# A delta rule and a SwiGLU block on one core: the products of chunk 2 in the merged form

## The chip, the cores and the metric

The kernel runs as one program on one core of one Trainium2 chip. The metric is the device time of an execution in microseconds (us). The kernel before was run three times: 691.24 us in the median, 690.71 to 693.55. A further execution was taken with the hardware profiler; every row of a profile below is from such an execution. The engines are called PE (TensorE, with PEld for its loading of weights), DVE (VectorE), ACT (ScalarE), POOL (GpSimd) and SP (SyncE, which issues the transfers). L961 is line 961 of the kernel.

## The reference

There are two blocks, one behind the other. The first is a delta rule over 4 × 8 heads, 768 tokens, head size 48. For each head a state S of 48 × 48 is carried from token to token:

```
k_n = k / (norm(k) + 1e-6)
for t in range(768):
    y[t]  = q[t] S
    S     = S + beta[t] * outer(k_n[t], v[t] - k_n[t] S)
```

The result y, with the heads of a token side by side, is x (3072 × 384). The second block is `(silu(x @ w_gate) * (x @ w_val)) @ w_out`, with 384 → 1536 → 384. All is f32.

## The kernel before

**Chunks.** The tokens are cut into NCH = 12 chunks of C = 64 tokens per head. Inside a chunk the recurrence becomes matrix products: K K and its inverse triangular system (made for two chunks at a time: `invert(g)`, joined by `join_1` or `join(g)`), P = the masked product Q K, and from the state S the products K S and Q S. Two heads' halves share the 128 partitions, so that one "product over all heads" is 32 small products (16 heads × 2 batches' halves); the trace shows each f32 product as two records, so 32 products stand as x64.

**The steps of a chunk.** `advance(c)` is a generator with four steps for c of 2 and above:

1. K S is subtracted from v (`vin`). For chunks below `MERGED` (L930, here 3) this is a product of 48 moving columns per head (L991) into the banks px; chunk 2 issues Q S (L944, `q_of_state`) right behind it into the banks py, and DVE subtracts in one instruction (L1001). For chunks from `MERGED` on, the moving operand is Q transposed and the state side by side (`qs`, 64 + 48 = 112 columns): one product per head (L961) gives K Q and K S together, par 0 into px, par 1 into py. DVE subtracts twice (L967) and masks K Q into P three times (L977: once from px, twice 64 partitions from py).
2. For chunks from `MERGED` on, Q S first (into py); then the first solution, `zt` times `r` (L1029, into px), which ACT copies out (`uu`, L1050).
3. The state's update (L1131, added by DVE at L1140) and P times u, which accumulates upon Q S in py (L1119); ACT copies y out (L1176, L1178).
4. y is transposed (L1192) into x of the chunk (`x_ffn`, L1198).

px and py are pairs of PSUM banks, one tile each; K K, K Q, the joins, the products above and the transposes all take turns in them. The other four banks (`ffn`) belong to the second block.

**P of a chunk below `MERGED`.** It is made ahead of the chunk, in `products(k_c, q_c)`, a generator of two steps that serves one chunk's K and one chunk's Q: in the first step both are transposed on PE, in the second `gram` makes K K of chunk `k_c` (L527 into px, copied by ACT at L553 and L556) and then, if `q_c < MERGED`, K Q of chunk `q_c` (L527 into py), which DVE masks (L545) into `p_sb`. Chunk 2's Q goes with chunk 4's K.

**The second block.** For chunks 0 and 1: gate and value products per pair of 128 columns (`gate_val`, L1397), silu on ACT (L1406), the product of both on DVE (L1408), and later the products with w_out (`output`, L1424). From chunk 2 on a form with fewer products is used (`gate_val_fast`, L1301; `output_fast`, L1507), with sums of weights and of x made on DVE (L1465, L1468). While chunks 0 and 1 run, DVE and ACT also convert the weights (`convert`, L289, L297, L309; `power_step`, L272, L278), which arrive in two words a value.

**The order.** It is written out by hand (`tc.manual_schedule`): each engine runs its instructions in the program's order. The second block's loops call `point(c)`, which runs one step: a step of `advance(c)` that has begun, or else a step of preparation (`prep_step`: a join, the second step of `products`, or a new one), or else the first step of `advance(c)`; `may_advance` lets a chunk begin when its P stands (`c in p_sb`) or, from `MERGED` on, its transposed Q (`c in qt`), and when enough steps of its join are done (two for chunk 2). `fill(n)` runs n units of work for DVE: conversions while there are weights left, then steps of `invert`. The list `spent`, in which steps enter what they take of DVE, is read in `point_and_fill` alone, which the products of chunks 2 and above call.

The last loop of the old form is `output(1, 1, fill, range(2, FT, 2))` (L1859): twelve products with w_out (`f`), and ahead of each even one from 2 on `fill(2)`, `point(2)` and `sums_of_w(f)`. The joins of chunk 2 and the steps of `advance(2)` stand there: ahead of f = 2 and 4 the two steps of the join (L809; L821 into py, which ACT copies out at L829), ahead of f = 6, 8 and 10 the first three steps of the chunk, and `finish(2)` behind the loop runs the fourth.

Of the kernel before, what the change touches and what calls it, by code (L numbers as in the profile page):

```python
# [20 lines left out]
def kernel(  # L21
# [539 lines left out]
    def gram(*args):  # L561
        for _ in gram_steps(*args):
            pass
# [363 lines left out]
        yield  # L927

    p_1 = []
    MERGED = 3  # L930

    def advance(c):

# [18 lines left out]

        if c >= MERGED:
            both = [
# [670 lines left out]
    def steps(kind, *args):  # L1625
        return gens.get((kind, args), (None, 0))[1]
# [4 lines left out]
    def products(k_c, q_c):  # L1631
# [6 lines left out]
        if k_c is not None:  # L1638
            gram(k_c, False, None, (nc.scalar.copy, nc.scalar.copy))
            if k_c % 2 == 1:  # L1640
                fills.append((k_c // 2, invert(k_c // 2)))
        if q_c is not None and q_c < MERGED:
            gram(q_c, True)
# [15 lines left out]
    def may_advance(c):  # L1659
        g = c // 2  # L1660
        due = {0: 0, 1: 2 + 2 * (c % 2)}.get(g, 2)
        return steps("advance", c) > 0 or ((c in p_sb or c >= MERGED and c in qt) and steps("join", g) >= due)

# [11 lines left out]
    def prep_step(c):  # L1675
# [19 lines left out]
        next(gen)  # L1695
        if k_c is not None or q_c < MERGED:
            going.append(gen)
# [206 lines left out]
```

## Time and profile before

| | us |
|---|---|
| three executions, median (lowest to highest) | 691.24 (690.71 to 693.55) |
| the profiled execution | 690.57 |
| its span, first to last instruction | 688.5 |
| PE busy in the span | 674.0 |
| DVE, ACT, POOL busy | 416.4, 261.6, 192.6 |
| granted clock of PE, mean | 0.996 of full |

A row of a timeline gives the start and the time it takes in us, the engine, the line, the operation, what it writes and reads, its shape and the number of instructions that the row holds; in brackets stands the idle time ahead of it and what ended that. PE's rows overlap a little, since its instructions are pipelined: the pace is read from one row's start to the next one's. "issue" is time in which the profile shows nothing that was waited for. The chain of waits gives start, length, engine and line of the work that ended last, followed back from the end.

### The profile page before, as it was taken

The page shows a single profiled execution, that of the slowest core. Times are in us where ns is not written, and L with a number is a line of the kernel's source. Part 1 is how long each engine was busy: PE and PEld are TensorE (multiplying, and loading weights), DVE is VectorE, ACT ScalarE, POOL GpSimd, SP SyncE. Part 2 cuts the span into 40 slices and gives each one's busy share as a digit, 9 for nine tenths or more (in the row PEclk, how much of TensorE's full clock was granted, in tenths as well). Part 3 has the DMA queues.
Part 4 walks back from the last instruction along what each step waited for, and adds up shares of the span by engine and source line. Part 5 has one row for each costly group of instructions (what it writes and reads, how often), then busy time and mean ns, then how long its engine had stood idle before and what let it go on. Part 6 is the DMA issues. An engine that isn't in the chain of part 4 may idle for free.

```text
span 688.5 us, 24321 instructions
## 1 busy us (share of the span) xinstructions
PE 674.0 (98%) x10696; PEld 627.2 (91%) x10696; DVE 416.4 (60%) x875; ACT 261.6 (38%) x554; POOL 192.6 (28%) x310
## 2 busy tenths in 40 slices
PE   8899999999999999999999999999999999999997
PEld 4687888667999999999999999999999999999997
DVE  7788788898667665637456556555554544433341
ACT  4776765214432622344233245242144142142230
POOL 5110031007882218810027830308810000000000
PEclk9999999999999999999999999999999999999999
DMA  9578733017650611554432373143143121221210
GB/s 133 147 195 217 222 104 126 13 29 175 136 112 11 131 60 40 112 100 92 95 72 70 74 135 71 55 109 71 56 109 70 55 64 47 56 63 47 73 43 24
DMA packets 143849, 62.23 MB, mean 90 GB/s; under 512 B 122976, under 2 KB 126048, under 8 KB 143744
## 3 DMA queue, kind: packets, MB, share of 16 engines
q1 hardware_dynamic: 141536, 60.19, 37.4%
q8 instruction: 84, 1.38, 0.8%
q10 hardware_dynamic: 2080, 0.39, 0.4%
q14 instruction: 21, 0.17, 0.1%
q0 software_dynamic: 128, 0.10, 0.1%
HBM read 53.58 MB, written 7.08 MB: 88 GB/s over the span
## 4 chain that ended last, share of the span: by engine, by line
PE 91%; ACT 2%; DMA 2%; SPq 2%; issue 1%; DVE 1%; POOL 0%; DVEq 0%; ACTq 0%; POOLq 0%
PE ffn L1301 43%; PE ffn L1507 20%; PE ffn L1397 9%; PE ffn L1424 4%; PE p_px L961 2%; PE p_py L944 2%; PE p_px L1029 2%; PE p_py L1119 1%; PE p_px L1131 1%; SPq L140 1%; DMA h_f<-in_moe_w_gate_dram 1%; PE p_px L527 1%; PE p_py L1192 1%; PE ffn L1058 1%; PE p_px L904 1%
## 5 line engine op out<-in xcount | busy, mean ns | idle before, releaser
L1301 PE MATMUL ffn<-x_ffn,wg_sb 128*128 128x128 f32 x840 | 128.4, 275 | 0.6 <-ACT ffn L1357 0.3
L1301 PE MATMUL ffn<-x_ffn,wv_sb 128*128 128x128 f32 x840 | 128.1, 275 | 0.0
L1301 PEld LDWEIGHTS ffn<-x_ffn,wg_sb 128*128 128x128 f32 x840 | 111.1, 192 | 1.0 <-ACT ffn L1357 0.7
L1301 PEld LDWEIGHTS ffn<-x_ffn,wv_sb 128*128 128x128 f32 x840 | 110.7, 192 | 0.0
L1336 DVE TENSOR_TENSOR h_f<-sil,ffn 128x256 f32<-128x256 f32 x120 | 49.6, 418 | 83.9 <-ACT sil L1331 82.5
L1331 ACT ACTIVATE sil<-ffn 128x256 f32<-128x256 f32 x120 | 46.0, 385 | 128.7 <-PE ffn L1301 126.6
L1507 PE MATMUL ffn<-wo_sb,h_f 128*128 128x192 f32 x480 | 83.4, 327 | 0.0
L843 POOL TENSOR_TENSOR n_b<-mb,half 128x32 f32<-128x32 f32 x5 | 30.1, 6010 | 178.6 <-DVE mb L569 178.6
L1507 PEld LDWEIGHTS ffn<-wo_sb,h_f 128*128 128x128 f32 x480 | 78.1, 190 | 0.3
L599 POOL TENSOR_TENSOR tmp<-zb,mb 128x31 f32<-128x31 f32 (+15 forms) x124 | 68.9, 556 | 16.9 <-DVE mb L586 7.5
L605 POOL TENSOR_TENSOR zb<-zb,tmp 128x31 f32<-128x31 f32 (+15 forms) x124 | 69.6, 561 | 9.7
L1468 DVE TENSOR_TENSOR ffn<-ffn,p_sb 128x512 f32<-128x512 f32 x58 | 40.3, 695 | 48.7 <-ACT ffn L1357 47.3
L1301 PE MATMUL ffn<-x_t,h_f 128*128 128x128 f32 x480 | 61.0, 280 | 0.2 <-ACT ffn L1314 0.2
L1301 PEld LDWEIGHTS ffn<-x_t,h_f 128*128 128x128 f32 x480 | 56.3, 191 | 2.1 <-ACT ffn L1314 0.4
L1468 DVE TENSOR_TENSOR o_sb<-o_sb,ffn 128x192 f32<-128x192 f32 x49 | 17.2, 352 | 63.6 <-PE ffn L1507 60.9
L1314 ACT COPY ffn<-ffn 128x512 f32<-128x512 f32 x30 | 17.1, 571 | 60.7 <-PE ffn L1301 60.7
L1465 DVE TENSOR_TENSOR h_f<-h_f,h_f 128x256 f32<-128x256 f32 x60 | 30.2, 509 | 11.4 <-PE ffn L1507 10.2
L1507 PE MATMUL ffn<-last_k,h_f 128*128 128x192 f32 x200 | 36.0, 327 | 0.0
L1397 PE MATMUL ffn<-x_ffn,wg_sb 128*128 128x256 f32 x144 | 34.5, 385 | 0.4 <-DVE x_ffn L1196 0.3
L1397 PE MATMUL ffn<-x_ffn,wv_sb 128*128 128x256 f32 x144 | 33.8, 382 | 0.0
L1507 PEld LDWEIGHTS ffn<-last_k,h_f 128*128 128x128 f32 x200 | 32.9, 190 | 0.1
L1397 PEld LDWEIGHTS ffn<-x_ffn,wg_sb 128*128 128x128 f32 x144 | 26.5, 190 | 4.8 <-DVE wg_sb L309 0.8
(314 smaller groups left out, 1123.1 us busy)
## 6 DMA issues: line engine op xcount, KB each, us to landing
h_f<-w_s SPq DMA_DIRECT2D x60, 256.0 KB, 2.8
p_sb<-w_s SPq DMA_DIRECT2D x27, 256.0 KB, 2.9
vin<-in_v_dram SPq DMA_DIRECT2D x48, 96.0 KB, 3.3
out_dram<-o_sb SPq DMA_DIRECT2D x48, 96.0 KB, 2.2
kn<-in_k_dram SPq DMA_DIRECT2D x20, 192.0 KB, 4.6
zt<-in_moe_w_out_dram SPq DMA_DIRECT2D x6, 384.0 KB, 4.0
qpad<-in_q_dram SPq DMA_DIRECT2D x36, 64.0 KB, 3.1
w_s<-h_f SPq DMA_DIRECT2D x7, 256.0 KB, 4.4
```

Source lines behind the costliest of these rows:

```text
L599: engine.tensor_tensor(out=t_v, in0=zb[:, 0 : j + 1, j : j + 1].to_broadcast([128, j + 1, m]), in1=mb[:, j : j + 1, j + 1 : R].to_broadcas ...
L605: engine.tensor_tensor(out=zb[:, 0 : j + 1, j + 1 : R], in0=zb[:, 0 : j + 1, j + 1 : R], in1=t_v, op=ALU.add,)
L843: nc.gpsimd.tensor_tensor(out=n, in0=mb.rearrange("p j i -> p (j i)")[:, 0 : R * R : R + 1], in1=half, op=ALU.pow,)
L1301: nc.tensor.matmul(p[:, u], w(u), moving, start=start and u == 0, stop=True, skip_group_check=True,)
L1314: nc.scalar.copy(p_y, p_x)
L1331: nc.scalar.activation(sil[:, n].rearrange("p (i n) -> p i n", i=2), p[:, 0:2], ACTF.Silu)
L1336: nc.vector.tensor_tensor(out=h_of(c, f, j), in0=sil[:, n].rearrange("p (i n) -> p i n", i=2), in1=p[:, 2:4], op=ALU.mult,)
L1397: nc.tensor.matmul(ps[name][:, i], w_sb[:, t, (f + i) * 128 : (f + i + 1) * 128], xts[c][:, t], start=(t == 0 and i == 0), stop=(t == KT - 1),
L1424: nc.tensor.matmul(p_o, hs[c, f - f % 2][:, f % 2, bp * 128 : (bp + 1) * 128], wo_sb[:, f], start=(f == 0), stop=(f == FT - 1),)
L1465: nc.vector.tensor_tensor(out=out, in0=a, in1=b, op=ALU.subtract)
L1468: nc.vector.tensor_tensor(out=out, in0=a, in1=b, op=ALU.add)
L1507: nc.tensor.matmul(p[x, part], a(f - f % 2)[:, f % 2], b(f), start=not begun and f == 0, stop=f == FH - 1, skip_group_check=True,)
```

## The change

Chunk 2 is computed in the merged form, as chunks 3 to 11 are:

```diff
--- before.py
+++ after.py
@@ -927,7 +927,7 @@
         yield
 
     p_1 = []
-    MERGED = 3
+    MERGED = 2
 
     def advance(c):
 
```

`MERGED` is read at four places. In `products`, K Q of chunk 2 is no longer made next to chunk 4's K K, nor masked. In `prep_step` it tells whether the second step of `products` is wanted; with chunk 4's K it is, before and after. In `may_advance`, chunk 2 asks for its transposed Q instead of its P. In `advance(2)`, the first step has the 32 products of 112 columns, two subtractions and three maskings in place of K S, Q S and one subtraction; Q S comes first in the second step, ahead of the first solution. What is computed stays the same.

## The prediction

> **What bounds the kernel now.** I read four views in this order: the page's busy times, the chain of waits, the timelines at the two places that the change touches, and the timeline at chunk 3, which already runs the form that chunk 2 is to get.
>
> ```profile
> PE 674.0 (98%) x10696; PEld 627.2 (91%) x10696; DVE 416.4 (60%) x875; ACT 261.6 (38%) x554; POOL 192.6 (28%) x310
> ```
>
> TensorE is busy for 674.0 of 688.5 us. That is an average, so the two places have to be looked at by themselves. After 171 us the waits of PE add up to only 1.6 us (its longest, 1.1 us, is one of L1301 for DVE): whatever shifts the work before 171 us shifts the end by as much. First place: the chain of waits where chunk 2's P is made today, near 76 us.
>
> ```profile
> 77.97 0.43 DVE wg_sb L309
> 78.40 0.04 issue
> 78.44 35.66 PE ffn L1397 x164
> ```
>
> The chain comes from DVE here, not from PE: the gate products of L1397 wait for a converted weight until 78.44 us and then run without a gap for 35.66 us (and PE stays in the chain to 155 us). The same place in DVE's timeline:
>
> ```profile
> 75.42 0.69 DVE L1408 TENSOR_TENSOR h_f<-sil,ffn 128x512 f32<-128x512 f32 x1 [4.13 <-PE ffn L1397]
> ...
> 78.64 1.28 DVE L545 TENSOR_TENSOR p_sb<-p_py,mask_q 128x512 f32<-128x512 f32 x2
> ```
>
> L1408 starts DVE's chain as soon as the value products end; the masking of P (L545) stands behind the conversion that PE waits for. Second place: the first two steps of chunk 2. First ACT's timeline, then PE's.
>
> ```profile
> 155.63 2.34 ACT L829 COPY zt<-p_py 32x512 f32<-32x512 f32 x4 [2.65 <-PE p_py L821]
> ```
>
> ```profile
> 156.91 1.15 PE L991 MATMUL p_px<-qs,kt 48*64 48x48 f32 x64
> 158.03 0.90 PE L944 MATMUL p_py<-qs 48*64 48x48 f32 x42
> 159.08 0.56 PE L944 MATMUL p_py<-qs 48*64 48x48 f32 x22 [0.16 <-issue]
> 159.57 1.56 PE L1424 MATMUL ffn<-wo_sb,h_f 128*128 128x384 f32 x4
> 161.05 1.15 PE L1029 MATMUL p_px<-vin,zt 64*64 64x48 f32 x64
> ```
>
> PE has no gap to speak of. K S (L991) writes px while ACT still copies out of py; Q S (L944) writes py from 158.03 us, just after the last of these copies ends (155.63 + 2.34 = 157.97). A f32 product stands as two records, so 32 products are x64. Third, chunk 3 in PE's and DVE's timelines:
>
> ```profile
> 193.52 0.31 PE L961 MATMUL p_px<-qs,last_k 48*64 48x112 f32 x1
> ...
> 195.21 2.05 PE L1301 MATMUL ffn<-x_t,h_f 128*128 128x128 f32 x16
> ...
> 199.87 1.15 PE L944 MATMUL p_py<-qs 48*64 48x48 f32 x64
> 200.84 1.11 PE L1029 MATMUL p_px<-vin,zt 64*64 64x48 f32 x64
> ```
>
> ```profile
> 195.33 0.55 DVE L967 TENSOR_TENSOR vin<-vin,p_px 128x384 f32<-128x384 f32 x1 [0.91 <-PE p_py L961]
> ...
> 196.98 1.39 DVE L977 TENSOR_TENSOR p_sb<-p_py,mask_q 64x512 f32<-64x512 f32 x2
> ```
>
> From the first merged product, PE is free after 195.21 - 193.52 = 1.69 us, DVE begins after 1.81 us, and its five instructions end at 196.98 + 1.39 = 198.37, 3.04 us after they began. In chunk 3 PE has 4.66 us of L1301 between the two steps, so nobody sees those 3.04 us.
>
> **The change, part by part.**
>
> *P by itself goes (76 us).* 32 products (x64) on PE, 1.1 us by L527's row at 76.22 us, and two masked copies on DVE, 1.28 us. The step that holds them also makes K K of chunk 4, so it stays a step, and the order of all later steps stays as it is; chunk 2 is let in by the join (two steps of it), not by P, so its start in the order stays too. On the path this is worth 0: PE would come to the gate products 1.1 us sooner, and wait 1.1 us longer for the weight that DVE finishes at 78.40 us. DVE cannot be sooner, for L1408 waits for products ahead of P. The 1.28 us stand behind that conversion, and PE has no wait for DVE from 78.44 to 151 us. The upper bound of the gain is the 1.1 us; I take 0, as the chain has it.
>
> *K S becomes the product of 112 columns (157 us).* It writes px and py in turn, so its second product needs py free, which K S did not: ACT's four copies (L829) hold py until 157.97. PE could begin at 156.91 + some 0.05 and stands until 158.03: 1.05 us of new waiting. Does the half that writes py's first bank have to wait for copies out of the second one too? The nearest row says yes:
>
> ```profile
> 20.78 1.09 PE L511 MATMUL p_py<-ident,last_k 128*128 128x128 f32 x8
> 21.91 1.07 ACT L515 COPY last_k<-p_py 128x512 f32<-128x512 f32 x2 [1.31 <-PE p_py L511]
> ```
>
> There the copy of py's first bank, whose transposes are the first four of eight, began only when all eight were done (20.78 + 1.09 = 21.87). The pair of banks is guarded as one. The Trainium skill (PSUM — Partial Sum Buffer, PSUM bank collisions raise a hardware error) says that guarding bank by bank and quadrant is enough; by that the first half could run under the copies, and the delay below would be 1.9 instead of 2.8 us. The row decides against that here.
>
> *DVE.* One subtraction (0.95 us, L1001) becomes two of 0.55 and three maskings of 0.68 to 0.70: 3.04 us by chunk 3. The merged product's last record ends at 158.03 + 1.77 = 159.80, less some 0.03 for the pair that ran ahead; DVE runs from 159.82 to 162.86. Behind it in DVE's queue stand eight sums of weights (159.30 to 162.07 now, 2.7 us): they end near 165.6, ahead of the state's addition (L1140), which then waits for PE until about 167.5. So they cost nothing; without those 1.9 us of cover they would delay the state. SP stores some of these sums: it is at 167.34 us when it issues the last three, and their sources are done by 165.6, so no transfer is later by more than the shift itself.
>
> *Q S moves behind the masking (second step).* It writes py, so it waits for both maskings that read py: 162.86 + 0.05 = 162.91. PE has only the four records of L1424 (1.49 us) to do meanwhile: 159.70 to 161.19. It stands 1.72 us. Q S then takes 200.84 - 199.87 = 0.97 us, and the first solution (L1029) starts at 163.87 instead of 161.05.
>
> *Sum.* Work of PE between 156.91 and L1029: before 1.12 + 1.54 + 1.48 us, after 1.69 + 1.49 + 0.97, so nothing (4.14 against 4.15). Waits: 1.05 + 1.72 = 2.77. L1029 is later by 2.82 us. Behind it come, now as before, copy, products, y's copies, transposes, x, all in one chain to 171 us, where PE goes on without gaps. **Plus 2.8 us**: the profiled execution's 690.57 us (span 688.5 and 2.1 around it) becomes 693.4. The median shown, 691.24, lies 0.67 above that execution, so the median after is 691.24 + 2.8 = **694.0 us**, 0.4% slower. Bounds of the delay: 1.9 with each bank guarded by itself, less 1.1 if P's 1.1 us count in full, so 0.8; above, 2.8 plus a lost stretch of clock, next.
>
> **The rivals.**
>
> *A slower clock (slower).* PE stands twice within 6 us, the second time for 1.72 us with only 0.3 us of work in the 2 us from 161 on. The trace has one drop: the granted clock is 0.54 from 14 to 16 us, after two microseconds in which PE was busy 0.74 us. Against: from 28 to 30 us it was busy only 0.66 us and the clock stayed 1.00. The drop lasted 3.41 us. L511's transposes went from 272 to at most 447 ns, so in 3.41 us 3.41 × 272 / 447 = 2.08 us of work gets done: 1.3 us lost. Time: 691.24 + 2.8 + 1.3 = 695.4. It decides if the granted clock is under 1.00 anywhere between 160 and 168 us. The Trainium skill (TensorE: Matmul & The Clock Gate, What's actually happening) has the clock halved after an idle window of about 3.4 us that runs freely; the drop's length agrees, and by an entirely idle window neither stand here would suffice.
>
> *Banks guarded one by one (less slower).* The first half runs from 156.97, the second from 158.03 in 0.83 us, DVE 158.95 to 161.99, Q S at 162.04, L1029 at 163.0: plus 1.9, 693.2 us. Against it the row of L515.
>
> *P's removal counts after all.* If PE were not held at 78.44, the 1.1 us would come off: plus 1.7, 692.9 us. The chain speaks against it. To be faster than before, the removed 1.1 and 1.28 us would both have to count and the two waits to vanish (−2.4, 688.8); no row supports it.
>
> **How the numbers follow.** A difference under 0.5% (3.5 us) is about what a measurement of this kernel cannot tell from none. Chances: the plain sum 0.66, the clock 0.18, the two smaller delays 0.12, faster 0.04. The plain sum lies only 0.7 us under the bound, and a stall for instructions in the dense run of Q S and L1029 (0.16 us in the row above, 0.64 us at 47.21 in the same kind of run), or the spread of executions, carries it over: I give 0.30 of its 0.66 to "slower by over 0.5%" and 0.36 to "within". So slower 0.30 + 0.18 = 0.48, within 0.36 + 0.12 = 0.48, faster 0.04. The range takes in 692.9 and 695.4 and some spread of the median: 692.6 to 696.2.
>
> **What would show it.** Right: PE still held until about 78.4 us by L309, with the wait grown to about 1.5 us; L961's second record at about 158.0, behind L829; Q S behind L977 at about 162.9 after an idle PE of 1.7 us; L1131 at about 166.4 instead of 163.62, and the same 2.8 us at every later stage. Wrong: if PE reaches the gate products' third weight before 78.3, if L961 runs through from 157.0, if Q S begins before the maskings end, if the clock falls below 1.00, or if the distance to the kernel before changes after 171 us.

## The result, and the profile after

The kernel after takes 697.93 us in the median of 8 executions (695.05 to 702.89), the kernel before, run between them, 692.11 us (690.71 to 693.57). The ratio is 1.0082, with a 95% interval of 1.0054 to 1.011: slower, by about 5.7 us. The forecast was 694.0 us and its range ended at 696.2, so twice the forecast delay came. The profiled execution of the kernel after took 697.05 us, with a span of 695.3 us against the 688.5 us of the kernel before: 6.7 us more.

The page's busy times say nothing about it; PE has 64 products and as many loads fewer, and is yet busy for 1.1 us more (675.1 against 674.0):

```profile
PE 675.1 (97%) x10632; PEld 626.7 (90%) x10632; DVE 416.2 (60%) x877; ACT 261.2 (38%) x554; POOL 192.9 (28%) x310
```

**The first place, near 76 us.** PE's timeline and the chain of waits of the kernel after:

```profile
77.03 1.16 PE L527 MATMUL p_px<-kt 64*64 64x64 f32 x64
78.12 1.13 PE L1397 MATMUL ffn<-x_ffn,wg_sb 128*128 128x256 f32 x4
80.23 1.99 PE L1397 MATMUL ffn<-x_ffn,wg_sb 128*128 128x256 f32 x8 [0.98 <-DVE wg_sb L309]
```

```profile
79.75 0.43 DVE wg_sb L309
80.18 0.04 issue
80.23 9.98 PE ffn L1397 x45
```

K K (L527) is followed at once by the gate products, which then stand for 0.98 us until DVE's conversion L309 ends at 80.18. K K starts 1.79 us later than in the trace of before (77.03 against 75.24), and the products held by L309 are released 1.79 us later as well (80.23 against 78.44). So nothing is won there. These 1.79 us arose in the part of the program that both kernels share. A second profiled execution of the kernel after stands 0.18 us ahead of the kernel before at 65 us, where this one is 1.79 us behind: it is a difference between executions and not the change.

**The second place, chunk 2.** PE's timeline of the kernel after (the shape behind the names, then xcount, and in brackets the idle time ahead), and below it ACT's and DVE's:

```profile
158.45 0.40 PE L961 MATMUL p_px<-qs,kt 48*64 48x112 f32 x2
159.56 0.31 PE L961 MATMUL p_py<-qs,kt 48*64 48x112 f32 x1 [0.70 <-ACT zt L829]
...
161.25 1.56 PE L1424 MATMUL ffn<-wo_sb,h_f 128*128 128x384 f32 x4
164.51 1.15 PE L944 MATMUL p_py<-qs 48*64 48x48 f32 x64 [1.71 <-DVE p_sb L977]
165.48 1.46 PE L1029 MATMUL p_px<-vin,zt 64*64 64x48 f32 x64
166.86 2.83 PE L1424 MATMUL ffn<-wo_sb,h_f 128*128 128x384 f32 x4
169.63 0.94 PE L1131 MATMUL p_px<-uu,kn 64*48 64x48 f32 x64
```

```profile
157.17 2.34 ACT L829 COPY zt<-p_py 32x512 f32<-32x512 f32 x4 [2.06 <-PE p_py L821]
```

```profile
161.41 0.56 DVE L967 TENSOR_TENSOR vin<-vin,p_px 128x384 f32<-128x384 f32 x1 [1.17 <-PE p_py L961]
...
163.07 1.39 DVE L977 TENSOR_TENSOR p_sb<-p_py,mask_q 64x512 f32<-64x512 f32 x2
```

Both forecast waits are there. The first product goes to px and the second, to py, starts when ACT's copies end (157.17 + 2.34 = 159.51). DVE's five instructions end at 163.07 + 1.39 = 164.46, 3.05 us after they began (forecast 3.04), and Q S follows at 164.51, after 1.71 us of standing (forecast 1.72). Then there is something that the sum did not hold: L1424, whose four records took 1.56 us before, takes 2.83, and the 64 records of L1029 take 1.46 instead of 1.15. The view by stretches shows why (length, then PE, PEld, DVE, ACT and POOL busy, the granted clock, the DMA's share, GB/s):

```profile
162.64:166.06 3.42, 1.71 (x105) 1.55 (x108) 3.34 (x8) 0.00 (x0) 3.42 (x2) 1.00 0.64 143
166.06:169.47 3.41, 3.41 (x41) 1.88 (x32) 1.20 (x4) 0.80 (x1) 0.39 (x1) 0.50 1.03 382
```

The clock is halved for 3.41 us behind a stretch of the same length in which PE was busy for half the time.

The starts of the same instructions in both profiled executions, in us, give the whole account:

| instruction | before | after | later by | what came in between |
|---|---|---|---|---|
| K K of chunk 4, L527 | 75.24 | 77.03 | 1.79 | shared part of the program, spread |
| gate products behind L309 | 78.44 | 80.23 | 1.79 | P's products gone: 0 |
| copies of the join, L829 | 155.63 | 157.17 | 1.54 | |
| first solution, L1029 | 161.05 | 165.48 | 4.43 | the two waits: 2.89 |
| state's update, L1131 | 163.62 | 169.63 | 6.01 | halved clock: 1.58 |
| join, L918, first of two | 241.17 | 247.15 | 5.98 | nothing for 75 us |
| chunk 4's L1119 | 299.03 | 305.47 | 6.44 | a stall inside L918: 0.46 |
| join, L918, second of two | 338.18 | 343.57 | 5.39 | a stall of before is gone: −1.05 |
| end of the span | 688.54 | 695.25 | 6.72 | a stall inside L918: 1.33 |

The last column is a difference of starts; the idle time that the profile puts ahead of one product is shorter (0.28 us of the 0.46, 1.14 of the 1.33). The last three rows lie more than 70 us behind the last instruction that the change touches. In PE's timeline of the kernel before, and then of the kernel after:

```profile
299.03 1.11 PE L1119 MATMUL p_py<-uu,p_sb 64*64 64x48 f32 x64
301.20 1.02 PE L1301 MATMUL ffn<-x_ffn,p_sb 128*128 128x128 f32 x7 [1.05 <-DVE qs L1140]
```

```profile
305.47 1.11 PE L1119 MATMUL p_py<-uu,p_sb 64*64 64x48 f32 x64
306.52 1.16 PE L1301 MATMUL ffn<-x_ffn,p_sb 128*128 128x128 f32 x8
...
343.57 1.17 PE L918 MATMUL p_py<-t,z 32*32 32x32 f32 x115
345.88 0.32 PE L918 MATMUL p_py<-t,z 32*32 32x32 f32 x13 [1.14 <-issue]
```

The kernel before stands for 1.05 us behind chunk 4's L1119; the kernel after does not, but stands for 1.14 us in the middle of 128 equal products of the join, where nothing is waited for. The prediction read the first of these as "one of L1301 for DVE", as the row has it. It is of another kind, as follows.

**Stalls at the border of a block of instructions.** Number PE's records from the start of the program: loads, products and the 125 entries of its sequencer (waits, above all) that the trace holds. The 1.05 us stand at record 10433, the 1.14 us at record 11457; divided by 256, each leaves a remainder of 193. (A product with its load and its wait is up to three records, so the product that the timeline shows behind the stall can be one or two later.) The DMA view has two queues that carry nothing but instructions; one of them moves 16 KB a packet (packets, MB, share of the engines):

```profile
q8 instruction: 83, 1.36, 0.8%
```

PE's 21389 records hold 83 places with the remainder 193, as many as there are packets; the kernel before has 21517 records, 84 such places and 84 packets, and the two counts are equal in every kernel below too. That this queue feeds PE is concluded from these counts. In each of these stalls the packet ahead landed 1.3 to 1.6 us before PE went on. So the theory: PE's program arrives in blocks of 256 records, and PE stalls at a border (a record with the remainder 193) when it gets there before the next block is usable. The change takes 64 loads and 64 products out of the program at 76 us, and moves every border behind it by half a block.

### The profile page after: what moved, and what is told of

Its sections match the earlier page's. It is cut to its first block, busy times and chain, and to the rows that moved or that the text cites. A ratio compares the mean times of both kernels' runs of the same rounds, so it can differ in the third digit from the quotient of the medians.

```text
span 695.3 us, 24196 instructions
## 1 busy us (share of the span) xinstructions
PE 675.1 (97%) x10632; PEld 626.7 (90%) x10632; DVE 416.2 (60%) x877; ACT 261.2 (38%) x554; POOL 192.9 (28%) x310
## 4 chain that ended last, share of the span: by engine, by line
PE 90%; ACT 2%; DMA 2%; SPq 2%; DVE 2%; issue 1%; POOL 0%; DVEq 0%; ACTq 0%
PE ffn L1301 42%; PE ffn L1507 20%; PE ffn L1397 9%; PE ffn L1424 4%; PE p_px L961 2%; PE p_py L944 2%; PE p_px L1029 2%; PE p_px L1131 1%; PE p_py L1119 1%; SPq L140 1%; DMA h_f<-in_moe_w_gate_dram 1%; PE p_px L527 1%; PE p_py L1192 1%; PE ffn L1058 1%; PE p_py L918 1%
## 5 line engine op out<-in xcount | busy, mean ns | idle before, releaser
L1301 PE MATMUL ffn<-x_ffn,wg_sb 128*128 128x128 f32 x840 | 128.4, 275 | 0.5 <-ACT ffn L1357 0.3
L1301 PE MATMUL ffn<-x_ffn,wv_sb 128*128 128x128 f32 x840 | 128.1, 275 | 0.0
L1301 PEld LDWEIGHTS ffn<-x_ffn,wg_sb 128*128 128x128 f32 x840 | 111.1, 192 | 1.0 <-ACT ffn L1357 0.7
L1301 PEld LDWEIGHTS ffn<-x_ffn,wv_sb 128*128 128x128 f32 x840 | 110.7, 192 | 0.0
L1301 PE MATMUL ffn<-x_t,h_f 128*128 128x128 f32 x480 | 61.0, 280 | 0.2 <-ACT ffn L1314 0.2
L1301 PEld LDWEIGHTS ffn<-x_t,h_f 128*128 128x128 f32 x480 | 56.3, 191 | 2.1 <-ACT ffn L1314 0.4
```

The costliest lines, as they stand in the source:

```text
L1301: nc.tensor.matmul(p[:, u], w(u), moving, start=start and u == 0, stop=True, skip_group_check=True,)
```

## The experiments

**The kernel after again, and with PE kept busy in the two waits.** The first kernel is the changed one without an edit. The second adds products that nobody reads (into a bank of the second block, ffn2), one ahead of the merged products, two ahead of Q S:

```diff
+        def keep_busy(n):
+            for _ in range(n):
+                nc.tensor.matmul(ffn_banks[2][:, 0:DM], ident, wo_sb[:, 0])
...
+            if c == 2:
+                keep_busy(1)
...
+            if c == 2:
+                keep_busy(2)
```

This kernel and the next two use a bank of the second block without setting its last 128 columns anew, and a part of chunk 2's result differs for it; the kernels further below that use the bank write these columns too. Apart from what the edits show, the instructions are the same.

> The changed kernel once more, to see what varies. Theory (two waits and the clock): against the kernel before, L1029 starts 2.8 to 2.9 us later than the start of L829 would make it in every execution (1.05 us for ACT's copies of py, 1.72 us for DVE's maskings), and a stretch of halved clock of 3.41 us behind them costs up to 1.6 us more in some executions and nothing in others; so the times spread by 2 us or more, and the median ratio is 1.004 to 1.008. Rival (the layout of the program): the loss is made of stalls for instructions and of the start, spread over the whole span, and is there before 75 us too; then the profile shows less than 2 us of loss between 150 and 171 us.

> The changed kernel with three products more that nobody reads, 128x384 as those of L1424 (0.75 us each): one ahead of the merged product, two ahead of Q S, so that PE works while it would wait. They fit into the two waits (0.75 of 1.05 and 1.49 of 1.72 us), and the waits stay. Theory: no halved clock between 155 and 175 us, L1424's four records take 1.5 us there and not 2.8, the median falls by the clock's share, 1 to 1.6 us, and stands 2.8 us (ratio 1.004) above the kernel before, with a spread like that one's (3 us). Rival (the clock was chance, or drops whatever PE does): the same time and spread as the changed kernel, ratio 1.008.

The kernel after again: 1.0074 (1.0043 to 1.0105), 696.99 us. Kept busy: 1.0052 (1.0024 to 1.0079), 695.91 us. In the profile of the first the waits are the same and the clock is not halved near 165 us, although PE stood for 1.70 us; but a stall stands inside chunk 2's L1119, at record 5313, which leaves 193 as well:

```profile
164.28 1.15 PE L944 MATMUL p_py<-qs 48*64 48x48 f32 x64 [1.70 <-DVE p_sb L977]
...
168.53 0.74 PE L1119 MATMUL p_py<-uu,p_sb 64*64 64x48 f32 x34
170.31 0.68 PE L1119 MATMUL p_py<-uu,p_sb 64*64 64x48 f32 x30 [1.03 <-issue]
```

So the halved clock comes in some executions and not in others. With PE kept busy it is not halved there either, L1029 is later by 2.89 us as without the extra products (here and below counted from the start of the join's copies, L829), and a stall of 0.43 us stands in the same run of L1119. The intervals of the two kernels overlap, so what the clock costs on average these runs do not tell. Both kernels also stall in the second L918 (0.85 and 0.57 us).

**Q S into a bank of its own, then the join's second step too.** In the first kernel chunk 2's Q S and P times u go into ffn0 and ffn2, so that Q S need not wait for the maskings; in the second the join's step (L821) goes there as well, so that the merged products need not wait for L829:

```diff
+        if c == 2:
+            p_y_of = [ffn_banks[n][:, 0 : NB * NJ * D].rearrange(...) for n in (0, 2)]
...
-                    p_y[half_of(b ^ par), par, bp, j],
+                    p_y_of[par][half_of(b ^ par), bp, j],
```

and in the second kernel also

```diff
-        p_j = ps_pair("p_j", tags[1]).rearrange("p e (m i) -> p e m i", i=C)
+        if c == 0:
+            p_j = [ffn_banks[n].rearrange("p (m i) -> p m i", i=C) for n in (0, 2)]
```

> The changed kernel with chunk 2's Q S, and P times u upon it, in two banks of the second block that are free then (ffn0 and ffn2) in place of py, so that Q S needs no masking to be done. Theory: the wait of 1.72 us ahead of Q S goes, L1029 then waits at most for the masking out of px; the first wait (1.05 us) stays; with only one short wait the clock stays full; L1029 about 1.1 to 1.3 us later than in the kernel before, ratio 1.0015 to 1.002. Rival (layout): the same loss as the changed kernel, ratio 1.008.

> As the run with Q S apart, and the second step of chunk 2's join in the same two banks too, so that the merged product need not wait for ACT's copies out of py (L829). Theory: both waits go and the clock stays full; L1029 within 0.3 us of its place in the kernel before, ratio 0.999 to 1.001; then the merged form itself costs nothing and all of the loss is the two waits and what they do to the clock. Rival (layout, or DVE's 3.04 us are the cost wherever they stand): ratio 1.004 or more.

Q S apart: 1.0032 (1.0015 to 1.0049), 693.95 us; L1029 is later by 1.11 us, the first wait alone. Both apart: 1.003 (1.0015 to 1.0045), 694.45 us; L1029 is within 0.3 us of before. Both ratios lie above what was expected, the second clear of it. So each wait goes when its bank is another. Between the kernel after again and Q S apart the ratio falls by 0.42%, where the second wait alone is 1.71 us or 0.25%; their intervals just overlap. But with no wait left the kernel is still 0.3% slower, some 2 us. PE's timeline of the kernel with both apart shows where they are:

```profile
167.41 0.74 PE L1132 MATMUL ffn<-uu,p_sb 64*64 64x48 f32 x34
169.12 0.67 PE L1132 MATMUL ffn<-uu,p_sb 64*64 64x48 f32 x30 [0.97 <-issue]
...
342.06 1.17 PE L922 MATMUL p_py<-t,z 32*32 32x32 f32 x115
344.36 0.32 PE L922 MATMUL p_py<-t,z 32*32 32x32 f32 x13 [1.14 <-issue]
```

They are the records 5313 and 11457 again, after the same 34 and 115 products of their runs, and the 1.05 us of before at 300 us are gone: 0.97 + 1.14 − 1.05 = 1.06 us, about half of the 2 us. Start to start, with short pauses near 243 and 247 us, it is more: this profile stands 2.97 us behind the one of before at L1029 and 5.19 us at the end, so 2.2 us came behind L1029. With Q S apart the stall in L918 is 1.67 us, and the clock is halved behind it:

```profile
340.02:343.43 3.41, 1.74 (x132) 1.59 (x129) 0.68 (x2) 0.33 (x1) 0.00 (x0) 1.00 0.58 77
343.43:346.84 3.41, 3.41 (x19) 3.41 (x18) 2.39 (x3) 1.06 (x2) 0.21 (x1) 0.50 0.60 106
```

**The removed records put back, unread.** The changed kernel, with the 32 products K Q of chunk 2 still issued at 76 us and read by nobody. The waits stay; from chunk 2's second step on, every border lies where it lay before the change:

```diff
+    def idle_gram(n):
+        p_v = [... for p in banks("p_g", "py")]
+        for bp, j, par, b, _ in list(every())[:n]:
+            nc.tensor.matmul(p_v[par][half_of(b), bp, j],
+                kt[2][half_of(par), bp, j, b], qt[2][half_of(par), bp, j, b])
...
+        elif q_c == 2:
+            idle_gram(32)
```

> The changed kernel, with the 32 products that the change takes away near 76 us still issued there (into py, read by nobody, no masking), where PE waits for DVE anyway. From the end of chunk 2's second step on, PE has then issued as many instructions as in the kernel before. Theory (blocks of instructions: 128 records fewer shift the borders of the fetched blocks into other dense runs of small products): the gap inside chunk 2's L1119 (0.4 to 1.0 us, or hidden by a slow clock) and the one inside L918 near 344 us (0.6 to 1.7 us) are gone, the gap behind chunk 4's L1119 near 300 us (1.05 us in the kernel before) is back; L1029 is still 2.8 to 2.9 us late; ratio 1.004 to 1.006 against 1.0074 to 1.0082 for the changed kernel. Rival (the gaps come from the waits or the merged form): the same gaps as in the changed kernel, the same ratio.

1.0034 (1.0021 to 1.0048), 695.05 us. With more work the changed kernel is faster, not slower: 1.0082 and 1.0074 without these products, 1.0034 with them, a little below the 1.004 to 1.006 expected (the interval of the first, from 1.0054, lies apart; that of the second just overlaps; the runs from here on are from another chip, where the kernel before was run in between as well). L1029 is later by 2.89 us, so what is left is the waits. The stalls in chunk 2's L1119 and in L918 near 344 us are gone, and the one behind chunk 4's L1119 is back, shorter, as before under the name of DVE:

```profile
303.67 1.11 PE L1130 MATMUL p_py<-uu,p_sb 64*64 64x48 f32 x64
305.23 1.13 PE L1312 MATMUL ffn<-x_ffn,p_sb 128*128 128x128 f32 x8 [0.44 <-DVE qs L1151]
```

**Both together.** No wait (as both apart) and next to no shift (as just now); a small product behind Q S (L1013) sets ffn2's last columns anew, which shifts the borders by four records:

> Both waits taken away (Q S and the join's second step of chunk 2 in ffn0 and ffn2) and the 32 unread products kept near 76 us; one small product more behind Q S (128 columns of ffn2, read by nobody). Theory (waits, clock and blocks are all of the loss): ratio 0.9985 to 1.0015, L1029 within 0.5 us of its place in the kernel before, gaps of PE behind 150 us as in the kernel before. Rival (something of the merged form is still dearer): 1.003 as without the unread products.

1.0004 (0.9986 to 1.0022), 692.61 us: the time of the kernel before. One stall of 0.41 us stands in chunk 2's join, at record 4801. The one of 1.05 us behind chunk 4's L1119, which was expected back, is not there, although the borders lie only four records off: L1148 (L1119's place) runs through, and so does the join near 340 us:

```profile
156.66 0.21 PE L836 MATMUL ffn<-t,d_o 32*32 32x32 f32 x1 [0.41 <-issue]
...
301.14 1.11 PE L1148 MATMUL p_py<-uu,p_sb 64*64 64x48 f32 x64
302.18 1.16 PE L1330 MATMUL ffn<-x_ffn,p_sb 128*128 128x128 f32 x8
...
339.22 1.29 PE L933 MATMUL p_py<-t,z 32*32 32x32 f32 x128
```

This is the main result: the slowdown has two parts that can each be undone by itself, the waits (1.0034 where they alone are left) and the shift (1.003 where it alone is left), and undone together nothing is left that can be measured. The last step by itself, from 1.003 to 1.0004, is not clear of the intervals, which overlap; what tells the two apart is where the stalls stand. It is no better than the kernel before either, and none of the versions tried was. Their sum, 0.64%, stands against the 0.74 and 0.82% of the changed kernel.

**P's work taken out of the kernel before, and nothing else.**

```diff
             for bp, j, par, b, _ in every():
+            if of_q and c == 2:
+                continue
```

> The kernel before, with chunk 2's K Q and its two maskings left out and nothing else changed (chunk 2 then uses chunk 1's P, so the output is another from chunk 2 on). It prices the removal by itself. The prediction's step: 0, since PE waits for DVE until 78.4 us in either case; the wait there grows by about 1 us. Theory of the blocks: the removal alone shifts the borders, so there are other gaps behind 150 us than in the kernel before, worth between -1 and +1.5 us in the sum, and none of it at 76 us. Rival (P's 1.1 us count): 1.1 us faster from 80 us on, ratio 0.9985.

1.0007 (0.9989 to 1.0026), 694.01 us against 692.78: no gain from 1.1 us less on PE and 1.28 us less on DVE. PE's timeline shows the same wait for L309 as in the kernel after, and two stalls of blocks in chunk 2:

```profile
79.39 1.99 PE L1401 MATMUL ffn<-x_ffn,wg_sb 128*128 128x256 f32 x8 [0.98 <-DVE wg_sb L309]
```

```profile
162.91 0.66 PE L1033 MATMUL p_px<-vin,zt 64*64 64x48 f32 x26 [0.58 <-issue]
...
167.46 0.67 PE L1123 MATMUL p_py<-uu,p_sb 64*64 64x48 f32 x30 [0.97 <-issue]
```

A third, of 1.17 us, stands in L918 at 341.4 us, and that of before at 300 us is gone. By these rows the kernel should be 0.58 + 0.97 + 1.17 − 1.05 = 1.67 us slower (0.24%), which the interval still holds. The ratio alone would also allow that P's removal wins a little and the stalls take it back; the row of 79.39 is what speaks against that. This kernel has the same shift as both apart and no waits, and its ratio is 1.0007 against 1.003: how much the shift costs in the median is known only roughly.

**Padding and a busy PE.** The padded changed kernel, with unread products in the waits once more, to ask again for the clock:

> The changed kernel with the 32 unread products near 76 us and with unread products in both waits (one of 384 columns ahead of the merged product, one of 384 and one of 512 ahead of Q S), so that neither the clock nor the blocks differ much from the kernel before and only the two waits are left. Theory: L1029 2.8 to 2.9 us late, no halved clock between 155 and 175 us, ratio 1.003 to 1.005 and a spread like that of the kernel before. Rival (the clock has no part): the same as the changed kernel with the unread products near 76 us alone.

1.0028 (1.0003 to 1.0053), 694.93 us, against 1.0034 without the unread products in the waits. No halving near 165 us, in either profile. The three products more are twelve records, and a stall of 0.50 us stands at record 5313 again, in chunk 2's state's update. The share of the clock is not settled by this pair: 0.06% lies far inside both intervals.

**Half of the padding.** Both waits away, and 16 of the 32 unread products: the borders move by a quarter of a block.

> Chunk 2 in the merged form with both waits taken away as in both_apart, and 16 of the 32 unread products K Q of chunk 2 issued at 76 us. Every record of PE behind 76 us stands 64 places later in the program than in both_apart and 64 earlier than in pad_both. Theory of blocks (PE stalls where a block of 256 records ends, at the record with remainder 193, where the run of products is dense): record 5313 is then the work that is record 5249 of both_apart, in the state's update of chunk 2, some 0.7 to 1.7 us earlier in the work than there but still in a dense run; so a gap of 0.4 to 1.0 us in the run of the state's update. Record 11457 is the work that is record 11393 of both_apart, still in L918's run of the join: a gap of 0.6 to 1.7 us there. Near 300 us the border falls among L1301's large products: no gap. Ratio to the kernel before between 1.0015 and 1.004, as both_apart (1.0030), and above pad_both (1.0004). Rival (the removed work itself matters, or the unread products help in proportion to their number): gaps at the same work as in both_apart, not at remainder 193, and a ratio half way, some 1.0017. The two ratios alone would hardly be told apart; the places of the gaps tell.

1.0002 (0.9975 to 1.0029), 693.3 us. In PE's timeline the first border is where the count puts it, 34 of the timeline's products earlier in the work than with both apart (16 unread ones and the small one are 68 records, 34 products and their loads), at the very first product of L1148, record 5313 again. The expectation named the state's update (L1160 here), which ends right ahead of it:

```profile
166.17 0.94 PE L1160 MATMUL p_px<-uu,kn 64*48 64x48 f32 x64
167.95 1.15 PE L1148 MATMUL ffn<-uu,p_sb 64*64 64x48 f32 x64 [0.85 <-issue]
```

That refutes the rival by which the stall belongs to the work and not to its number. Near 300 us there is no stall, as expected. But the stall expected in the join near 341 us did not come, and two came that were not expected, at borders as well: 0.77 us at 172.94 us in a join (L820) and 0.85 us at 541.73 us in another (L933). The ratio lies below what was expected, though its interval reaches into it. So "a dense run at a border" was too simple a rule for *whether* a border stalls.

**What decides at a border.** All eleven profiles together answer that. From 90 us on they hold 760 borders (records with the remainder 193). For each, take the time from the border before to this one, the stall itself included, and any gap at the border. The first table's limit of 5.2 us was set with the result in view, just above the longest such time that has a stall, 5.10 us:

```
256 records took      borders   with a gap over 0.3 us
under 5.2 us              199   20   (0.41 to 1.67 us)
5.2 us and more           561    0

kernel      record   256 records took   gap    block landed ahead of the record
before       10433        2.81 us      1.05          1.45 us
after        11457        3.96         1.14          1.33
again         5313        4.54         1.03          1.61
both apart    5313        4.55         0.97          1.41
both apart   11457        3.96         1.14          1.46
half padded   5313        4.29         0.85          1.40
half padded  11457        5.54         none          3.59
```

Every gap of PE of more than 0.35 us behind 100 us that is not one of the two waits of chunk 2 is among the twenty. In all twenty the block's packet landed 1.24 to 1.61 us before the record; where a short block passed without a gap, the packet had mostly landed earlier, in the median 2.6 us ahead. None of the 760 borders was passed sooner than 1.24 us after its packet had landed, which points to a better form of the rule: PE stalls when it would pass a border sooner than some 1.2 to 1.6 us after the landing. The border that let the half-padded kernel pass is the last row: there the 256 records held more of the large products and took 5.54 us. These conditions were found after that run and from the same profiles; no run was made to test them.

The profiles also give the shift a price without the medians. From the start of chunk 2's L1029, behind both waits, to the end, each needs more or less time than the profile of before (us, by how far its borders were moved):

```
by 116 to 128 records          +1.48 (again)   +1.52 (kept busy)   +2.21 (both apart)   +2.90 (without P)
  with a halved clock as well  +2.29 (after)   +3.54 (Q S apart)
by 60 records                  +1.32 (half padded)
by 12, 4 or 0 records          -0.38 (padded, busy)   -1.11 (both together)   -0.24 (padded)
```

It is one execution of each, but with a full clock all whose borders were moved by 60 records or more are slower by 1.3 us or more, and none with the borders at or near their old places is slower at all.

## Why the prediction was right and wrong

- *P by itself is worth nothing.* Right. The place of the gate products against L309 is the same to 0.01 us in both profiles, and the kernel without P's work alone is not faster. The new wait for L309 is 0.98 us; I wrote 1.5, counting a wait into it that the kernel before hardly has.
- *The merged product waits for L829, and the pair of banks is guarded as one.* Right: 159.56 is 0.05 us behind the last copy. Only the very first pair ran ahead, so the rival of banks guarded one by one is out.
- *Q S waits for the maskings.* Right to 0.01 us (1.71 us), and DVE's five instructions to 0.01 us. L1029's growth is 2.89 us against 2.82. The Trainium skill (PSUM — Partial Sum Buffer, PSUM bank collisions raise a hardware error) would have had 1.9 us by guards for each bank; the trace decided for the pair, as the row of L515 had told.
- *It passes through to the end.* Right for the waits: from L1131 to 241 us the delay stays at 6.0 us, and the padded changed kernel, in which little more than the waits is left, is slower by 0.34%, 2.4 us.
- *The sum, plus 2.8 us.* This is the step that failed. It held waits and work, and nothing for the place of an instruction in the program, and it took for granted that a shift of 2.8 us at 171 us is one of 2.8 us at the end. "Work of PE sums to nothing" is true of the busy time, but 128 records fewer move all later borders of blocks by half a block. Where the shift alone is left it costs 0.30% (0.15 to 0.45%), about 2 us; the profile of that kernel has 2.2 us of it behind L1029, its long gaps half of that. The size is less sure than the place: the kernel without P's work, with the same shift, is slower by 0.07% (−0.11 to 0.26%) only, and to put the records back takes 0.40 to 0.48% off the changed kernel. I had seen such stalls ("a stall for instructions", 0.16 and 0.64 us) and entered them as spread that might carry the sum over a bound, not as a term that the change moves. And the 1.05 us at 300 us I read as a wait for DVE, because the row names DVE; chunk 4's L1140 is merely the last thing that had ended.
- *"Wrong if the distance to the kernel before changes after 171 us".* That test did its work: it changed three times (0.46, −1.05, 1.33), at places the change does not touch.
- *The slower clock, given 0.18.* In the profiled execution this rival came, and cost 1.58 us instead of the estimated 1.3: its stretch held L1424's products, which took 1.8 times as long, and not transposes. (The estimate also divided the time that single transposes took, 272 by 447 ns; from start to start they came every 0.21 us in that stretch instead of 0.11, which would have made it 1.7.) In the second profile of the same kernel it did not come. The Trainium skill (TensorE: Matmul & The Clock Gate, What's actually happening) says that an idle window of about 3.4 us, which runs freely, halves the clock; the 3.41 us agree, but the window ahead was not idle: PE was busy for 1.71 of its 3.42 us. I had let "entirely idle" weigh against this rival; the rows say otherwise. What it adds to the median stays open, with an estimate below.

Put together, for the median: 0.34% of waits and 0.30% of borders are 4.4 us of the 5.1 to 5.7 us that the two series show. The rest is inside the intervals. The clock is a candidate for it: the mean granted clock was 0.9960 over the 15 executions of the changed kernel and 0.9972 over 78 of the kernel before, by which I estimate 0.9 us more of lost clock (0.1 to 1.6). No run separates it, so it is not a shown cause.

## What to carry to other kernels

Where the busiest engine runs long rows of small products, the number of instructions ahead of a stage can itself change its time: a change that removes some has to be priced with where the block borders come to lie, and a control with the same count of unread instructions separates the two. When a difference between two profiles grows far behind the last line that was changed, look there for gaps in the middle of equal instructions before looking for a wait. And a merged product that saves an instruction's work is no gain where its second output bank and its longer reading by the next engine stand on the path: here 32 products fewer bought two waits, of 2.9 us together.

## What the runs showed of the hardware

- By the counts of all eleven profiles, PE's program comes in packets of 16 KB, one for 256 records, through a queue for instructions. A border stalled PE by 0.4 to 1.7 us, only where it came less than 5.2 us after the border before (20 of 199 such borders, none of the 561 others). PE went on 1.24 to 1.61 us after the packet had landed, and never sooner at any of the 760.
- The profile may put such a stall down to whatever engine ended last: the 1.05 us "for DVE" in the kernel before are gone wherever the borders moved, by four records already, with DVE's work as before.
- The clock was halved for 3.41 us behind windows in which PE was busy for 50% (the kernel after) and 51% (Q S apart) of the time. Behind one with 54% it was not:

```profile
162.81:166.23 3.42, 1.86 (x126) 1.86 (x128) 3.35 (x9) 0.00 (x0) 3.21 (x2) 1.00 0.90 223
166.23:169.64 3.41, 3.27 (x127) 2.28 (x121) 1.18 (x4) 0.80 (x1) 0.00 (x0) 1.00 1.01 373
```

These rows are of the padded changed kernel, whose waits are the same as those of the kernel after. Three windows do not make a threshold: in these and the other profiles windows busy for 43 to 58% passed without a halving, and near the start some of up to 63% were followed by one.
